# Sliding-window attention and a cosine-gated MLP on one core: the first pair of heads of q and k comes as f32 through SyncE's queue and is cast on chip

## Chip, cores and metric

One core of a Trainium2 chip runs the whole kernel. The metric is the device time of one execution in microseconds, lower is better: 307.88 us as the median of three runs of the kernel before (307.68 to 308.02).

## What is computed

Attention over 8 batches, 8 heads, 576 positions and 64 channels per head, causal, with a window of 64 positions; then an MLP on the 4608 tokens of 512 channels.

```python
scores = scale * np.matmul(q, k.transpose(0, 1, 3, 2))
mask = (rel >= 0) & (rel < window)            # rel = query position - key position, window = 64
attn = softmax(where(mask, scores, -1e9))
x = np.matmul(attn, v)  ->  [4608, 512]
h = x @ w_in                                  # 512 -> 2048
g = h * np.cos(h)
out = (g @ w_out).astype(np.float32)          # 2048 -> 512
```

All inputs are f32 in DRAM; the kernel computes in bf16 with f32 sums.

## The kernel before

**Two halves.** The MLP works on nine token tiles of 512 (`mt`); each needs 64 first-layer matmuls (L351) and 64 second-layer matmuls (L522). The attention for a batch is computed in units of 64 queries against 128 keys and is laid between the matmuls of the MLP, at places given by a plan of due times. Only the attention of batch 0 has nothing to hide behind: its steps are written out by hand in the string `FIRST` (L41 to L48) and are issued in that order, one after the other, each to its engine. Every engine then works through its own list in order, and waits where an operand isn't there yet. A schedule is not found by the compiler: the order in which the program is written is the order on each engine.

**The first stage.** The heads of batch 0 are taken in four pairs. A row tile `rows` holds q and k of batch 0 as bf16, 64 rows per head with nine positions each. For pair `p`, in the names of `FIRST`:

- `load_heads` (L140, DMA at L142) brings q or k of the pair from DRAM on GpSimd's queue. The source is f32 and the tile bf16, so this DMA casts on its way.
- `tq.p`, `tk.p` (L186): 18 small TensorE transposes each of q and k from `rows` into PSUM, through the identity `ident`.
- `pq.p`, `pk.p` (L197/L199 for q, L109 for k): the transposed rows are copied to the tile `T` by VectorE (d) or ScalarE (a).
- `s.p.g` (L238, L244): the scores of four units. One matmul puts the mask (`mask16` through `ident`, L238) into the PSUM bank, eight small ones add q times k (L244).
- `m` (L273, VectorE: row maximum), `e` (L288, ScalarE: four exponentials with their sums), `i` (L295, VectorE: reciprocal), `n` (L302, GpSimd or VectorE: normalisation), `w` (L311, TensorE: transposes of the weights), `c` (L109: copy of those), `v` (L330: weights times values), `x` (L109: copy to `xT`), `h` (L351: first matmuls of the MLP), `tb` (L346: ScalarE's table for the sine).

**The mask** is made on chip: GpSimd writes position differences by two iotas (`put_steps`, L115), VectorE makes the three mask pieces from them in five instructions (`put_masks`, L119 to L123; step `mk`), and ScalarE casts these to `mask16` in three (L125). Both parts of `mk` are therefore in the lists of VectorE and ScalarE ahead of the first `pq` and `pk`.

**The loads** before `FIRST` are in the order q and k of pair 0, the iotas, q and k of pairs 1, 2 and 3, and four pieces of v, all on GpSimd's queue. SyncE's queue carries no load: its first instruction in the kernel before is the DMA at L170, which copies values on chip for batch 1, at 45.8 us.

**Output buffers.** The pool `moe` has three buffers with the tag `out` (128 x 2 x 512 f32), for the results of the MLP (`out_sb`, L514). The first of them is needed when the second layer of token tile 0 is copied out.

The part that sets up the first stage (L447 to L457):

```python
    nc.vector.memset(small, 0.0)
    exp_table()
    make_identity(nc, ident)
    load_heads("q", 0, 0, 1)
    load_heads("k", 0, 0, 1)
    put_steps()
    for p0, n in ((1, 1), (2, 1), (3, 1)):
        for name in ("q", "k"):
            load_heads(name, 0, p0, n)
```

Of the kernel before, what the change touches and what calls it, by code (L numbers as in the profile page):

```python
# [14 lines left out]
F32 = mybir.dt.float32  # L15
# [15 lines left out]
RC = 9  # L31
# [20 lines left out]
def kernel(  # L52
# [9 lines left out]
    nc = tc.nc  # L62
    B, H, S, D = q.shape
    assert (B, H, S, D) == (8, 8, 576, 64)
    scale = 1.0 / math.sqrt(D)
    d_model = H * D
# [9 lines left out]
    moe = ctx.enter_context(tc.tile_pool(name="moe", bufs=2))  # L76
# [31 lines left out]
    def copy(engine, out, in_):  # L108
        {"a": nc.scalar.copy, "p": nc.gpsimd.tensor_copy}.get(engine, nc.vector.tensor_copy)(out, in_)  # L109
# [3 lines left out]
    def put_steps():  # L113
        for h in range(2):
            nc.gpsimd.iota(mask[64 * h:64 * h + 64, 0], pattern=[[2, 128]], base=-65, channel_multiplier=-2,  # L115
                           allow_small_or_imprecise_dtypes=True)
# [11 lines left out]
    def halves(tile_):  # L128
        return {name: tile_[:, i * PAIRS * S:i * PAIRS * S + PAIRS * S].rearrange("p (a x) -> p a x", a=PAIRS)
                for i, name in enumerate(("q", "k"))}  # L130

    def rows(b):
        return rowtiles[1 if b == 1 else 0]
# [6 lines left out]
    def load_heads(name, b, p0=0, n=PAIRS):  # L140
        src = {"q": q, "k": k}[name][b, 2 * p0:2 * p0 + 2 * n]
        nc.gpsimd.dma_start(out=halves(rows(b))[name][:, p0:p0 + n],  # L142
                            in_=src.rearrange("(a h) (p c) d -> (h p) a (c d)", h=2, c=RC))
# [198 lines left out]
    def exp_table():  # L342
        nc.scalar.activation(small, small, AF.Exp, scale=0.0)  # L343
# [45 lines left out]
    n = n_first  # L389
# [56 lines left out]

    nc.vector.memset(small, 0.0)  # L447
    exp_table()
    make_identity(nc, ident)
    load_heads("q", 0, 0, 1)  # L450
    load_heads("k", 0, 0, 1)
    put_steps()
    for p0, n in ((1, 1), (2, 1), (3, 1)):
        for name in ("q", "k"):
            load_heads(name, 0, p0, n)
    for c in range(4):
# [108 lines left out]
```

## Time and profile before

| | |
|---|---|
| median of three runs | 307.88 us (307.68 to 308.02) |
| the profiled execution, its own time | 308.04 us |
| its span (first to last instruction) | 306.0 us |
| TensorE matmul busy | 294.1 us, 96% of the span |
| ScalarE, VectorE, GpSimd busy | 235.6, 219.3, 171.9 us |
| first matmul starts | 4.82 us |
| first matmul of the MLP (`h.0`) | 21.68 us |
| start of the unbroken row of MLP matmuls (`h.2`) | 26.21 us |

The profile lists instructions by engine and by line of the kernel. "PE" is TensorE's matmul, "PEld" its weight load, "DVE" VectorE, "ACT" ScalarE, "POOL" GpSimd, "SP" SyncE. A row of the timeline has the start in us from the span's start, the busy time in us (instructions that follow each other directly are merged, with their count), engine, line, operation, output and input, and in brackets the idle time before it with what ended it. The chain of waits is the work that ended last, followed back from the last instruction to what released each step. Busy times of TensorE overlap a little, since matmuls are pipelined; where a step's length matters the distance from start to start is used.

### The profile page before, as it was taken

How to read it: one execution, taken by the hardware profiler on the slowest of the kernel's cores; microseconds unless marked ns; L12 is line 12 of the kernel's file. 1: busy time of each engine (PE TensorE's matmuls, PEld its weight loads, DVE VectorE, ACT ScalarE, POOL GpSimd, SP SyncE). 2: the span in 40 equal slices, each digit the busy share in tenths (PEclk: the TensorE clock that was granted, in tenths of full speed). 3: DMA queues.
4: the chain of work that ended last, by engine and by line, in shares of the span. 5: the costliest groups of instructions: out<-in, count | busy, mean ns of one | idle time of the engine just before them, and what ended most of it. 6: DMA issues, size and time to landing. Idle time of an engine off the chain costs nothing.

```text
span 306.0 us, 7884 instructions
## 1 busy us (share of the span) xinstructions
PE 294.1 (96%) x2668; PEld 143.1 (47%) x2668; DVE 219.3 (72%) x832; ACT 235.6 (77%) x786; POOL 171.9 (56%) x200
## 2 busy tenths in 40 slices
PE   3979999999999999999999999999999999999996
PEld 2645444444444444444454445444544454454443
DVE  2796889678787778777878787788778877235701
ACT  4798689977997799879986998699869987106600
POOL 8997237889465976497759765957533630000000
PEclk9989999999999999999999999999999999999999
DMA  6999999599969999999999999999993441011012
GB/s 83 167 211 207 208 168 161 79 179 166 238 110 159 180 197 135 164 149 219 145 170 161 213 141 170 161 216 120 171 170 117 88 130 61 0 72 70 0 69 71
DMA packets 165577, 43.58 MB, mean 142 GB/s; under 512 B 154720, under 2 KB 161056, under 8 KB 165536
## 3 DMA queue, kind: packets, MB, share of 16 engines
q0 software_dynamic: 99632, 18.36, 75.4%
q1 hardware_dynamic: 65760, 24.52, 39.9%
q8 instruction: 21, 0.34, 0.5%
q10 hardware_dynamic: 144, 0.20, 0.2%
q14 instruction: 20, 0.16, 0.2%
HBM read 36.70 MB, written 9.44 MB: 151 GB/s over the span
## 4 chain that ended last, share of the span: by engine, by line
PE 83%; ACT 5%; DVE 5%; DMA 3%; POOL 1%; issue 1%; POOLq 0%; DVEq 0%
PE h_ps L351 41%; PE out_ps L522 33%; ACT e L288 3%; PE o_ps L330 3%; PE s_ps L261 3%; DMA rows<-in_q_dram 1%; PE out_ps L366 1%; DVE s L277 1%; DMA wT<-w 1%; DVE negm L273 1%; DVE w L302 1%; ACT L343 1%; PE tk_ps L186 1%; PE tq_ps L186 1%; POOL w L302 1%
## 5 line engine op out<-in xcount | busy, mean ns | idle before, releaser
L351 PE MATMUL h_ps<-xT,w_in 128*128 128x512 bf16 x576 | 128.1, 381 | 0.9 <-ACT xT L109 0.5
L522 PE MATMUL out_ps<-w_out,gT 128*128 128x512 bf16 x560 | 125.1, 379 | 0.2 <-DVE gT L510 0.2
L510 DVE TENSOR_TENSOR gT<-h_ps,sin 128x512 bf16<-128x512 f32 x144 | 95.5, 689 | 35.4 <-ACT sin L507 35.2
L507 ACT ACTIVATE sin<-h_ps 128x512 f32<-128x512 f32 x144 | 83.0, 599 | 34.2 <-PE h_ps L351 33.0
L288 ACT ACTIVATE e<-s,negm 128x128 f32<-128x128 f32 x256 | 98.6, 387 | 0.3 <-DVE negm L277 0.3
L302 POOL TENSOR_TENSOR w<-e,rden 128x512 bf16<-128x512 f32 (+1 forms) x76 | 74.3, 992 | 32.4 <-DVE rden L295 30.3
L351 PEld LDWEIGHTS <-w_in 128*128 128x128 bf16 x576 | 55.9, 98 | 66.7 <-issue 2.0
L522 PEld LDWEIGHTS <-gT 128*128 128x128 bf16 x560 | 53.2, 98 | 62.4 <-issue 0.2
L277 DVE CUSTOM_DVE_ANT_0 s<-s_ps,mask 128x128 f32<-128x128 f32 x256 | 58.1, 285 | 0.4 <-PE s_ps L261 0.4
L288 ACT ACTIVATION_READ_ACCUMULATOR e<-s,negm 128x1 f32 x256 | 48.0, 188 | 0.0
L149 POOL DMA_DIRECT2D rows<-in_q_dram x30 | 25.4, 866 | 25.3 <-DMA T<-rows 15.5
L162 POOL DMA_DIRECT2D v<-in_v_dram x35 | 29.6, 869 | 12.4 <-DMA rows<-in_k_dram 5.8
L109 ACT COPY out_sb<-out_ps 128x512 f32<-128x512 f32 (+1 forms) x18 | 10.1, 561 | 24.4 <-PE out_ps L522 19.0
L295 DVE RECIPROCAL rden<-den 128x4 f32<-128x4 f32 (+1 forms) x80 | 13.8, 172 | 18.3 <-ACT e L288 17.1
L149 POOL DMA_DIRECT2D rows<-in_k_dram x30 | 25.5, 898 | 0.5 <-DMA T<-rows 0.5
L109 DVE CAST xT<-o_ps 128x512 bf16<-128x512 f32 x26 | 16.9, 681 | 6.5 <-PE o_ps L330 6.2
L277 DVE DVE_READ_ACCUMULATOR2_ANT negm<- 128x1 f32 x256 | 21.3, 83 | 0.0
L109 DVE COPY out_sb<-out_ps 128x512 f32<-128x512 f32 x18 | 12.4, 689 | 12.0 <-PE out_ps L522 12.0
L288 ACT ACTIVATE e<-s_ps,negm 128x128 f32<-128x128 f32 x32 | 11.4, 394 | 1.6 <-DVE negm L273 1.4
L261 PE MATMUL s_ps<-T 64*64 64x128 bf16 x512 | 12.1, 221 | 0.0
L261 PEld LDWEIGHTS <-T 64*64 64x64 bf16 x512 | 8.2, 106 | 8.3 <-DVE negm L277 3.9
L330 PEld LDWEIGHTS <-v 128*64 128x64 bf16 x504 | 9.7, 114 | 4.4 <-issue 2.3
(54 smaller groups left out, 148.9 us busy)
## 6 DMA issues: line engine op xcount, KB each, us to landing
out_dram<-out_sb SPq DMA_DIRECT2D x16, 512.0 KB, 6.9
v<-in_v_dram POOLq DMA_DIRECT2D x28, 128.0 KB, 8.3
rows<-in_q_dram POOLq DMA_DIRECT2D x24, 128.0 KB, 5.9
rows<-in_k_dram POOLq DMA_DIRECT2D x24, 128.0 KB, 9.0
w_out<-in_moe_w_out_dram POOLq DMA_DIRECT2D x2, 1024.0 KB, 16.8
w_in<-in_moe_w_in_dram POOLq DMA_DIRECT2D x2, 768.0 KB, 12.1
wT<-w SPq DMA_TRANSPOSE x66, 3.8
out_dram<-out_sb SPq DMA_DIRECT2D x3, 256.0 KB, 2.0
```

Source lines behind the costliest of these rows:

```text
L109: {"a": nc.scalar.copy, "p": nc.gpsimd.tensor_copy}.get(engine, nc.vector.tensor_copy)(out, in_)
L149: nc.gpsimd.dma_start(out=rows(b)[lo:lo + n, slot * 512:slot * 512 + 512].rearrange("p (h d) -> p h d", h=H), in_={"q": q, "k": k}[name][b ...
L162: nc.gpsimd.dma_start(out=vt.rearrange("p (h d) -> p h d", h=H), in_=v[b, :, c * 128:c * 128 + n, :].rearrange("h p d -> p h d"))
L261: nc.tensor.matmul(out=s_ps[cross][to, u].rearrange("p (a t) -> p a t", a=2), lhsT=q_cols(b, p, j)[d], rhs=k_cols(b, p, j)[d], start=True, ...
L277: nc.vector.tensor_tensor_reduce(out=s[:, u], in0=s_ps[:, u], in1=mask[:, 2 - j % 2 if j else 0], scale=-scale if b else -1.0, scalar=BIG, ...
L288: nc.scalar.activation(e[:, u], s[:, u], AF.Exp, bias=negm[:, u:u + 1], scale=1.0 if n < n_first else -1.0, accum_out=den[:, u:u + 1])
L302: (nc.gpsimd if engine == "p" else nc.vector).tensor_tensor(out=w[:, 0:u], in0=e[:, 0:u], op=ALU.mult, in1=rden[:, 0:u].unsqueeze(2).to_br ...
L330: nc.tensor.matmul(out=o_ps[64 * h:64 * h + 64, 64 * i:64 * i + 64], lhsT=values_of(b)[:, max(j - 1, 0), 128 * p + 64 * h:128 * p + 64 * h ...
L351: nc.tensor.matmul(out=st["h", ff], lhsT=w_in_sb[:, ks, ff * 128:ff * 128 + 128], rhs=st["xT", mt][:, ks], start=start, stop=stop)
L507: nc.scalar.activation(sin, h_ps, AF.Sin, bias=math.pi / 2.0)
L510: nc.vector.tensor_tensor(out=gt[:, e], in0=h_ps, in1=sin, op=ALU.mult)
L522: nc.tensor.matmul(out=o_ps[e], lhsT=gT[ff // 2][:, ff % 2, ms * 128:ms * 128 + 128], rhs=w_out_sb[:, ff], start=ff == 0, stop=ff == n_ff - 1)
```

## The change

Nothing of the computation changes. Four edits stand in one place, behind `exp_table()`:

- q and k of pair 0 no longer come through `load_heads`. SyncE issues two DMAs, ahead of everything else in its list, that bring the same rows as f32 into two of the three `out` buffers (`first_f32`, 576 f32 to a partition).
- ScalarE casts q, and VectorE casts k, from `first_f32` to the place in `rows` that the DMA filled before. Both casts come ahead of the mask's steps in the lists of these engines.
- GpSimd loads pair 1 where it loaded pair 0, and has two DMAs less in all; the iotas stay behind its second load.
- Pairs 2 and 3 follow the iotas directly.

```diff
     nc.vector.memset(small, 0.0)
     exp_table()
+    first_f32 = {}
+    for name, src in (("q", q), ("k", k)):
+        first_f32[name] = moe.tile([128, 2, d_model], F32, tag="out", name="first_f32", bufs=3).rearrange("p a b -> p (a b)")[:, 0:S]
+        nc.sync.dma_start(out=first_f32[name], in_=src[0, 0:2].rearrange("h (p c) d -> (h p) (c d)", c=RC))
     make_identity(nc, ident)
-    load_heads("q", 0, 0, 1)
-    load_heads("k", 0, 0, 1)
+    load_heads("q", 0, 1, 1)
+    load_heads("k", 0, 1, 1)
     put_steps()
-    for p0, n in ((1, 1), (2, 1), (3, 1)):
+    for name, engine in (("q", "a"), ("k", "d")):
+        copy(engine, halves(rows(0))[name][:, 0], first_f32[name])
+    for p0, n in ((2, 1), (3, 1)):
         for name in ("q", "k"):
             load_heads(name, 0, p0, n)
```

The beginning of VectorE's list, with the difference marked. The rows at L119 to L123 make the mask, `rows_72` is the tile of batch 0's rows, and the branch into the program differs by its line number alone:

```order
-L560 UNCONDITIONAL_BRANCH
+L566 UNCONDITIONAL_BRANCH
 L447 MEMSET small 128x1
+L109 CAST rows_72<-first_f_87 128x576
 L119 TENSOR_TENSOR mask<-mask 128x128
 L120 TENSOR_SCALAR mask<-mask 128x128
```

The cast of k now stands in front of all the mask's instructions. The beginning of ScalarE's list, with the load of its exponential table and the three casts to `mask16` (L125):

```order
 L343 ACT_TABLE_LOAD
 L343 ACTIVATE small<-small 128x1
+L109 CAST rows_72<-first_f_85 128x576
 L125 CAST mask_81<-mask 128x384
 L125 CAST mask_81<-mask 128x256
```

The cast of q stands between the table and the mask's casts. GpSimd's list around the iotas, where each line at L142 is the load of one pair's q or k:

```order
 L142 DMA rows_72<-in_k_dram 128x576
 L115 IOTA mask 64x128 x2
-L142 DMA rows_72<-in_q_dram 128x576
-L142 DMA rows_72<-in_k_dram 128x576
 L142 DMA rows_72<-in_q_dram 128x576
 L142 DMA rows_72<-in_k_dram 128x576
```

Two loads have gone behind the iotas, and what follows them comes two DMA issues sooner. SyncE's list gains its two DMAs at the front. TensorE's list keeps its order; only its first weight load now waits for ScalarE and not for a DMA.

## Prediction

> **What bounds the kernel now.** I first read the chain of waits by engine, to see whether TensorE sets the end, and then the same chain in order of time, to see where it does not. Times in the rows are us from the span's start.
>
> ```profile
> PE 83%; ACT 5%; DVE 5%; DMA 3%; POOL 1%; issue 1%; POOLq 0%; DVEq 0%
> ```
>
> ```profile
> 1.45 1.29 POOL rows L142 x2
> ...
> 3.25 4.54 DMA rows<-in_q_dram
> ...
> 9.80 0.56 PE s_ps L244 x8
> ...
> 12.97 0.58 PE s_ps L244 x8
> ...
> 13.58 0.69 DVE negm L273
> ...
> 21.68 1.44 PE h_ps L351 x3
> ...
> 26.21 5.77 PE h_ps L351 x26
> ```
>
> TensorE sets 83% of the span. From 26.21 on it has work without a break, in an order that the change leaves alone. So the change is worth as much as it moves that 26.21. The chain behind it is: the load of q of pair 1 (issued at 3.25 as GpSimd's third load, landed 4.54 later), `tq.1` at 7.83, TensorE until `s.1.1` ends at 13.5, then VectorE with no gap until `h.0` at 21.68. ScalarE runs beside it: it waits 1.08 before 10.88 (row below), and afterwards is full.
>
> The timeline to 11.5 shows the steps that the change touches:
>
> ```profile
> 0.74 1.28 ACT L343 ACT_TABLE_LOAD   x1 [0.74 <-PEq L549]
> 3.25 0.55 POOL L142 DMA_DIRECT2D rows<-in_q_dram  x1
> 3.33 0.29 DVE L119 TENSOR_TENSOR mask<-mask 128x128 f32<-128x128 f32 x1 [2.46 <-POOL mask L115]
> 4.34 0.11 DVE L123 MEMSET mask<- 128x64 f32 x1
> 4.54 1.02 ACT L125 CAST mask<-mask 128x384 bf16<-128x384 f32 x3 [2.30 <-DVE mask L123]
> 4.82 0.69 PE L186 MATMUL tq_ps<-ident,rows 64*64 64x64 bf16 x18 [4.82 <-DMA rows<-in_q_dram]
> 5.49 0.69 PE L186 MATMUL tk_ps<-ident,rows 64*64 64x64 bf16 x18
> 6.11 0.61 PE L238 MATMUL s_ps<-mask,ident 128*128 128x512 bf16 x1
> 6.22 0.64 ACT L109 COPY T<-tk_ps 128x576 bf16<-128x576 bf16 x1 [0.66 <-PE tk_ps L186]
> 6.91 0.63 PE L244 MATMUL s_ps<-T 64*64 64x128 bf16 x8 [0.19 <-ACT T L109]
> 7.83 0.69 PE L186 MATMUL tq_ps<-ident,rows 64*64 64x64 bf16 x18 [0.29 <-DMA rows<-in_q_dram]
> 10.88 0.65 ACT L197 ACTIVATE T<-tq_ps 128x576 bf16<-128x576 bf16 x1 [1.08 <-PE tq_ps L186]
> 11.43 0.36 ACT L288 ACTIVATE e<-s_ps,negm 128x128 f32<-128x128 f32 x1
> ```
>
> Three facts matter. TensorE waits 4.82 for q of pair 0. The mask is ready at 4.54 + 1.02 = 5.56, only 0.55 before L238 needs it, so the mask is second in line. And the 0.29 before 7.83 is pair 1 arriving late.
>
> **The change part by part: pair 0's landing.** The price of a SyncE load of f32 from DRAM stands nowhere. The nearest rows are SyncE's last stores, with nothing beside them, its copies on chip in the midst of other traffic, and the loads of pair 0 and its followers on GpSimd's queue (columns: transfer, queue, count, KB, median us from issue to landing); and one issue by SyncE.
>
> ```profile
> out_dram<-out_sb SPq DMA_DIRECT2D x3, 256.0 KB, 2.0
> v<-v SPq DMA_DIRECT2D x1, 256.0 KB, 6.2
> out_dram<-last_sb SPq DMA_DIRECT2D x1, 64.0 KB, 1.6
> ```
>
> ```profile
> rows<-in_q_dram POOLq DMA_DIRECT2D x1, 144.0 KB, 3.3
> ```
>
> ```profile
> 303.30 0.33 SPq L370 DMA_DIRECT2D out_dram<-last_sb  x1
> ```
>
> From 64 to 256 KB the stores grow by 0.4, 2.1 ns per KB. The f32 tile is 288 KB, so about 2.0 + 0.07 = 2.07. SyncE should begin with the others (ScalarE's first row starts at 0.74), so q lands at 0.75 + 2.07 = 2.8. k is issued 0.33 later, at 1.08, and would land at 3.15 if it had the queue to itself; behind q's 288 KB (0.6 at the same slope, less the 0.33) it is 3.4. I take q at 2.8 and **k at 3.4**. Bounds for k: 1.08 + 1.6 = 2.7, and 1.08 + 6.2 = 7.3; the second is a copy amid full traffic, which the beginning doesn't have:
>
> ```profile
> 0.00:2.60 2.60, 0.00 (x0) 0.00 (x0) 0.06 (x1) 1.49 (x2) 1.86 (x8) 1.00 0.00 0
> 2.60:3.80 1.20, 0.00 (x0) 0.00 (x0) 0.43 (x2) 0.00 (x0) 1.14 (x5) 1.00 0.70 82
> ```
>
> The last two columns (share of the DMA engines, GB/s) are zero until 2.6, so SyncE's loads begin on idle engines and meet pair 1's loads only at their end.
>
> [...]
>
> **The casts.** Rows for both engines, f32 from SBUF (ScalarE's gives min, median and max in ns, VectorE's the mean in ns after the busy us):
>
> ```profile
> L125 ACT CAST mask<-mask x3: 293/400/512, 4.5 to 5.3; 128x384 bf16<-128x384 f32 x1, 128x256 bf16<-128x256 f32 x1, 128x128 bf16<-128x128 f32 x1
> ```
>
> ```profile
> L120 DVE TENSOR_SCALAR mask<-mask 128x128 f32<-128x128 f32 x1 | 0.2, 227 | 0.0
> L122 DVE COPY mask<-mask 128x64 f32<-128x64 f32 x1 | 0.2, 196 | 0.0
> ```
>
> ```profile
> L109 DVE COPY T<-tk_ps 128x576 bf16<-128x576 bf16 x3 | 2.3, 752 | 0.0
> ```
>
> ScalarE grows by 0.86 ns per element (293 at 128, 512 at 384), so 576 take 0.68. VectorE grows by 0.48 (196 at 64, 227 at 128), so 576 take 0.44; the upper bound is the 0.75 of the same width from PSUM. I take 0.45.
>
> **The new beginning.** q cast: 2.85 to 3.53 (ScalarE has its table since 2.02). `tq.0` at 3.6 instead of 4.82, `tk.0` ends 0.67 + 0.69 later, at 4.9. That 1.2 is *not* what is gained, since the cast of k stands ahead of the mask. k cast: 3.45 to 3.9, behind it VectorE's mask row, which took 4.45 − 3.33 = 1.12: 3.93 to 5.05, instead of 4.45. ScalarE's casts follow 0.09 later and take 1.02: ready at 6.16 instead of 5.56. `pk.0` then starts at 6.18 (before 6.22), the scores of L244 0.69 later at 6.87 (before 6.91). So TensorE waits for the mask from 4.9 to 6.2, and the first score comes when it came before. What does go is the wait behind it: pair 1 now lands where pair 0 did, 3.3 after issues at 1.45 and (in the middle of the 1.29 that the two take) about 2.1, by 5.5. `tq.1` follows L244's eight by their 0.56 in the chain: 7.43 instead of 7.83, a **gain of 0.4**.
>
> In general `tq.1` starts at k's landing + k's cast + 3.56 (0.04 + 1.14 + 0.09 + 1.02 + 0.02 + 0.69 + 0.56), and it pays as long as landing plus cast is below 4.27. If k lands by 2.9 the mask is no longer held up, and `pk.0` follows at 5.58: gain 1.0 at most (0.64 from the mask's 5.56, and the 0.36 behind L244).
>
> **What carries the 0.4 on.** Three rows from the end of the stage:
>
> ```profile
> 18.52 1.48 DVE L109 COPY v<-v 64x1536 bf16<-64x1536 bf16 x1
> ...
> 19.51 0.40 PE L311 MATMUL tw_ps<-ident,w 128*128 128x128 bf16 x4 [1.48 <-POOL w L302]
> ...
> 23.59 0.58 ACT L109 COPY wT<-tw_ps 128x512 bf16<-128x512 bf16 x1 [0.48 <-PE tw_ps L311]
> ```
>
> From `tq.1` to `s.1.1` TensorE has no gap, and pairs 2 and 3 are issued two DMAs (twice 0.55, so 1.1) earlier than before, so it isn't stopped by them. ScalarE's `pq.2` at 10.88 waits for `tq.2`, and from `e.0.0` at 11.43 ScalarE has no idle time until the 0.48 before 23.59, so until 23.11; it moves by 0.4 as one piece. VectorE's row from 13.58 starts when `s.1.1` ends, 0.4 earlier too. GpSimd has its two issues less and so 1.1 of slack; its `n.1.1`, for which TensorE waited 1.48 at 19.5, comes earlier, but VectorE was busy until 20.0 anyway (`z.0`), so I price that at nothing; without that cover it would be another 0.5 to 1. Two of the three output buffers are taken, but free again from 3.9, some 40 us ahead of their first use. SyncE has nothing else to do in the whole stage. The w_in pieces come earlier, not later. Sum: 308.04 − 0.4 = 307.64 for the profiled execution, which stood 0.16 above the median; on the median's footing **307.5**.
>
> **Rivals.** *The clock.* The same 18 transposes take 0.69 before 13.3 and less after it, and three MLP matmuls at 21.68 take 1.44 (26 take 5.77 later, 0.22 each):
>
> ```profile
> 13.33 0.49 PE L186 MATMUL tq_ps<-ident,rows 64*64 64x64 bf16 x18
> ```
>
> ```profile
> 6.60:10.00 3.40, 2.88 (x52) 2.00 (x53) 2.13 (x4) 1.76 (x9) 3.37 (x4) 1.00 1.08 159
> 10.00:13.40 3.40, 3.40 (x64) 2.40 (x62) 2.19 (x5) 2.52 (x13) 3.23 (x4) 1.00 2.04 163
> ...
> 16.80:20.20 3.40, 1.92 (x37) 1.16 (x35) 3.40 (x7) 3.40 (x20) 3.32 (x3) 1.00 1.18 215
> 20.20:23.70 3.50, 3.25 (x40) 1.98 (x37) 3.09 (x8) 2.91 (x16) 3.48 (x5) 0.51 1.15 208
> ```
>
> So TensorE was slow until about 13.4 (the clock's column, third from the right, shows 1.00 there; the durations say otherwise), fast after 3.4 us that it filled, and slow again (0.51) for 3.5 after 3.4 that it filled only to 1.92. Without the wait before 7.83, it fills the stretch 6.6 to 10.0, and might be fast 3.4 sooner. VectorE then gets `s.1.1` about 1 earlier; ScalarE, which still starts `e.0.0` on `m.0.0`, only about 0.5 to 0.6. The gain above that lies at the end: ScalarE's last copy at 23.59 waited 0.48 for slow TensorE work (it was free at 23.11). Together 0.9: **307.0**. The same price covers k landing by 2.9. [...]
>
> *k comes late (the slower side).* The cast of k holds the mask, and the mask all scores. If a load by SyncE takes the 3.3 of GpSimd's load, k lands at 4.4; with the cast, `tq.1` comes at 8.4, 0.6 later: 308.5; with the cast at 0.75, 308.8. It decides from landing plus cast over 4.27. For it: both loads share the engines with pair 1 from 2.6. [...] Against: they start on idle ones.
>
> *Nothing arrives.* The 0.4 is used up further on, where VectorE and ScalarE run neck and neck from 13.6 to 21.7, or by the slow stretch at 20.3 staying put and covering more of `h.0`: 307.9.
>
> **How the numbers follow.** A gain of 0.1 to 0.6, the forecast, 0.44; the clock or an early k (307.0) 0.31; late k 0.17; nothing 0.08. About 0.2% (0.62 us, below 307.26 or above 308.50) is what a measurement here can tell. Faster by that: most of the second case and a little of the first, 0.33; slower: most of the third, 0.16; within, the rest, 0.51. The range reaches to both sides: 306.6 (the 1.0 with some of the clock) to 308.6. The forecast's own range is 307.2 to 307.8.
>
> **What would show it.** First, the cast of k's start: below 3.8 it pays. `tq.0` near 3.6, then a gap in TensorE of about 1.3 before L238 at 6.2 that is ended by ScalarE's mask cast; no DMA wait before `tq.1`, at 7.4; `h.2` at 25.8. If `tq.1` has moved and `h.2` hasn't, my carrying on is wrong; if transposes before 13 take 0.5, the clock decided; if L238 starts after 6.9, k was late.

## The result, and the profile after

The changed kernel took **306.57 us** (median of 22 runs, 306.17 to 308.42), the kernel before 307.99 beside it (22 runs): a ratio of 0.9961 [0.9949, 0.9973], so 1.2 us less, with 0.8 to 1.6 in the interval. The profiled execution took 306.21 (span 304.3), 1.83 less than that of before, so part of its difference is the execution's own. The runs of one kernel spread by 1 to 2 us with the course of TensorE's clock, which differs between runs (a mean of 0.989 to 1.00 in the changed kernel's): where its mean was 1.00, the kernel before took 307.51 (mean of 18 runs, taken beside the experiments) and the changed one 306.32 (mean of 9), again 1.2.

The chain of waits by engine, and five pieces of the same chain in order of time:

```profile
PE 87%; ACT 6%; DVE 3%; DMA 1%; issue 1%; POOL 0%; SPq 0%; DVEq 0%; POOLq 0%; ACTq 0%
```

```profile
1.20 3.14 DMA first_f<-in_k_dram
...
5.94 1.02 ACT mask L125 x3
...
11.41 4.19 ACT e L288 x24
...
23.19 1.28 ACT L346
...
25.21 5.77 PE h_ps L351 x26
```

The chain now begins with the load of k, goes through the mask, and reaches `h.2` at 25.21, where it was 26.21: 1.00 earlier. From `pq.2` at 10.76 to 25.16 it is ScalarE's list, which has no wait in all that time. Its first pieces are the ones that I had worried about. Rows from the first 8 us of the changed kernel:

```profile
0.75 0.39 SPq L452 DMA_DIRECT2D first_f<-in_q_dram  x1
1.20 0.42 SPq L452 DMA_DIRECT2D first_f<-in_k_dram  x1
3.68 0.67 ACT L109 CAST rows<-first_f 128x576 bf16<-128x576 f32 x1 [1.43 <-DMA first_f<-in_q_dram]
4.36 0.46 DVE L109 CAST rows<-first_f 128x576 bf16<-128x576 f32 x1 [3.48 <-DMA first_f<-in_k_dram]
4.40 0.69 PE L186 MATMUL tq_ps<-ident,rows 64*64 64x64 bf16 x18 [4.40 <-ACT rows L109]
5.74 0.11 DVE L123 MEMSET mask<- 128x64 f32 x1
5.94 1.02 ACT L125 CAST mask<-mask 128x384 bf16<-128x384 f32 x3 [1.59 <-DVE mask L123]
6.86 0.63 ACT L109 COPY T<-tk_ps 128x576 bf16<-128x576 bf16 x1
7.01 0.59 PE L238 MATMUL s_ps<-mask,ident 128*128 128x512 bf16 x1 [1.44 <-ACT mask L125]
7.54 0.63 PE L244 MATMUL s_ps<-T 64*64 64x128 bf16 x8
7.95 0.71 PE L186 MATMUL tq_ps<-ident,rows 64*64 64x64 bf16 x18
```

k landed at 1.20 + 3.14 = 4.34, its cast held up the mask, TensorE waited 1.44 for that, and `tq.1` (last row) came at 7.95, **0.12 later than before**. By the part of the program that the prediction priced, the change should have lost a little. Where it won shows in GpSimd's list (and, in this one execution, in TensorE's clock as well; the iotas below tell the two apart). The timeline of GpSimd from the w_in loads to the last normalisation of batch 0, first of the kernel before:

```profile
10.11 1.50 POOL L175 DMA_DIRECT2D w_in<-in_moe_w_in_dram  x2
11.67 1.04 POOL L302 TENSOR_TENSOR w<-e,rden 128x512 bf16<-128x512 f32 x1
...
14.95 1.08 POOL L302 TENSOR_TENSOR w<-e,rden 128x512 bf16<-128x512 f32 x1
16.09 2.25 POOL L109 COPY v<-v 64x2048 bf16<-64x2048 bf16 x1
18.42 3.21 POOL L302 TENSOR_TENSOR w<-e,rden 128x512 bf16<-128x512 f32 x3
...
22.55 1.06 POOL L302 TENSOR_TENSOR w<-e,rden 128x512 bf16<-128x512 f32 x1
```

and of the changed kernel:

```profile
8.93 1.56 POOL L175 DMA_DIRECT2D w_in<-in_moe_w_in_dram  x2
10.81 1.04 POOL L302 TENSOR_TENSOR w<-e,rden 128x512 bf16<-128x512 f32 x1 [0.32 <-DVE rden L295]
...
14.09 1.08 POOL L302 TENSOR_TENSOR w<-e,rden 128x512 bf16<-128x512 f32 x1
15.23 2.33 POOL L109 COPY v<-v 64x2048 bf16<-64x2048 bf16 x1
17.64 3.21 POOL L302 TENSOR_TENSOR w<-e,rden 128x512 bf16<-128x512 f32 x3
...
21.77 1.06 POOL L302 TENSOR_TENSOR w<-e,rden 128x512 bf16<-128x512 f32 x1
```

In both, the list shows no wait from GpSimd's first load at 1.45 to the last of these rows, but for one of 0.32 in the second. (The page's busy share doesn't show it, since DMA issues aren't counted as busy.) Two issues less put the w_in rows 1.18 earlier, the new wait takes 0.32 of it, and the rest stays with every row down to the last normalisation, `n.3.0`: 22.55 to 21.77, **0.78 earlier**. TensorE waits for these rows: its wait of 1.48 before `w.1.1` at 19.51 is now one of 1.16 at 18.74, 0.77 earlier.

### The profile page after: what moved, and what is told of

The parts are those of the page before. It is cut to its first block, busy times and chain, and to the rows that moved or that the text cites. A ratio compares the mean times of both kernels' runs of the same rounds, so it can differ in the third digit from the quotient of the medians.

```text
span 304.3 us, 7887 instructions
## 1 busy us (share of the span) xinstructions
PE 291.6 (96%) x2668; PEld 141.7 (47%) x2668; DVE 218.5 (72%) x833; ACT 235.8 (77%) x787; POOL 171.1 (56%) x198
## 4 chain that ended last, share of the span: by engine, by line
PE 87%; ACT 6%; DVE 3%; DMA 1%; issue 1%; POOL 0%; SPq 0%; DVEq 0%; POOLq 0%; ACTq 0%
PE h_ps L351 41%; PE out_ps L528 37%; ACT e L288 4%; PE o_ps L330 3%; PE s_ps L261 3%; PE out_ps L366 1%; DMA first_f<-in_k_dram 1%; DVE s L277 1%; PE tq_ps L186 1%; ACT wT L109 0%; DVE w L302 0%; PE tk_ps L186 0%; DVE out_sb L109 0%; ACT L343 0%; ACT L346 0%
```

## The experiments

Four theories, with the letters that the expectations use. *First scores* (A): the stage is set by the arrival of the first pairs, `tq.1` above all (the prediction's). *The clock* (B): TensorE runs at full speed in other stretches than before. *GpSimd's list* (C): the two issues that GpSimd no longer makes. And, once two loads put back had cost the whole gain, *traffic* (D): the bytes of these loads, not their issues. Extra loads, iotas and matmuls of the experiments write tiles that nobody reads. "Ratio" is to the kernel before on the same chip, with its 95% interval.

**First scores: the mask ahead of the cast.** In the changed kernel the cast of k moves behind the mask's five instructions on VectorE.

```diff
-    "tq.0 mk tk.0 pq.0.d pk.0.a s.0.1 tq.1 tk.1 l s.0.0 m.0.1 pq.1.d tq.2 e.0.1 pk.1.d s.1.0 pq.2.a "
+    "tq.0 mk kc tk.0 pq.0.d pk.0.a s.0.1 tq.1 tk.1 l s.0.0 m.0.1 pq.1.d tq.2 e.0.1 pk.1.d s.1.0 pq.2.a "
-    for name, engine in (("q", "a"), ("k", "d")):
-        copy(engine, halves(rows(0))[name][:, 0], first_f32[name])
+    copy("a", halves(rows(0))["q"][:, 0], first_f32["q"])
...
+             "kc": lambda: copy("d", halves(rows(0))["k"][:, 0], first_f32["k"]),
```

> The changed kernel with one thing moved: VectorE's cast of k stands behind the five mask instructions instead of ahead of them. Theory A (the mask's row behind k's cast set the first scores): the mask is ready near 5.6 instead of 6.96, the first L244 starts near 6.4 instead of 7.54, tq.1 at the landing of pair 1 near 7.0 instead of 7.95, and h.2 follows by 0.5 to 0.9, for 305.6 to 306.1 us. Rival B (only TensorE's clock decides, the beginning is hidden): tq.1 moves as said, but the time stays within 0.3 of the changed kernel's 306.57. Rival C (the two loads fewer on GpSimd's queue give the gain): as B.

Measured 306.09, ratio 0.9939 [0.9926, 0.9952]. Three rows of its timeline:

```profile
6.35 0.63 PE L244 MATMUL s_ps<-T 64*64 64x128 bf16 x8 [0.16 <-ACT T L109]
...
15.35 0.40 PE L311 MATMUL tw_ps<-ident,w 128*128 128x128 bf16 x4 [1.76 <-POOL w L302]
...
21.67 1.06 POOL L302 TENSOR_TENSOR w<-e,rden 128x512 bf16<-128x512 f32 x1
```

The first scores come 1.19 sooner than in the changed kernel (`tq.1` at 6.73, 1.22 sooner), the end only 0.5 (0.7 by the ratios). TensorE gives the rest back as a wait of 1.76 for GpSimd, whose last row gains 0.10. So 1.2 at the first scores is worth some 0.5 to 0.7 here, and 0.12 lost there nearly nothing.

**The clock.** Small matmuls of the identity fill TensorE's gaps ahead of `tq.0`, `s.0.1` and `w.1.1`: 30, 1 and 18 in the kernel before (below; `g` is the step `warm`), 26, 12 and 18 in the changed one.

```diff
-    "tq.0 mk tk.0 pq.0.d pk.0.a s.0.1 tq.1 tk.1 l s.0.0 m.0.1 pq.1.d tq.2 e.0.1 pk.1.d s.1.0 pq.2.a "
+    "g.30.X1 tq.0 mk tk.0 pq.0.d pk.0.a g.1.X1 s.0.1 tq.1 tk.1 l s.0.0 m.0.1 pq.1.d tq.2 e.0.1 pk.1.d s.1.0 pq.2.a "
...
-    "s.3.0 s.3.1 c.0.1.d n.1.1.p c.0.0.d w.1.0 m.3.0 i.2.0 z.0.d c.1.0.a n.2.0.p w.1.1 c.1.1.d v.0 "
+    "s.3.0 s.3.1 c.0.1.d n.1.1.p c.0.0.d w.1.0 m.3.0 i.2.0 z.0.d c.1.0.a n.2.0.p g.18.X0 w.1.1 c.1.1.d v.0 "
...
+    def warm(n, which):
+        t = bank(which, "warm_ps")
+        for _ in range(n):
+            nc.tensor.matmul(out=t[:, 0:128], lhsT=ident, rhs=ident, start=True, stop=True, skip_group_check=True)
```

> The kernel before, with 49 matmuls of the identity by itself (128 wide, results unused) laid where TensorE waits: 30 ahead of tq.0, 1 ahead of s.0.1, 18 ahead of w.1.1. They remove no load and no cast. Rival B (the clock): TensorE is at full speed from about 8 on and stays there, transposes take 0.45 to 0.5 us per 18 instead of 0.69, the slow stretch at 20.3 is gone, and the time falls by 0.9 to 1.5, to 306.5 to 307.1, with less spread. Theory A or rival C: TensorE's speed is hidden behind ScalarE and VectorE, 307.7 to 308.0.

> The changed kernel with 56 such matmuls: 26 ahead of tq.0, 12 ahead of s.0.1, 18 ahead of w.1.1. If the clock (B) is the whole difference, it stands within 0.3 us of the kernel before with the same filling, and its slower runs near 308.2 vanish. If the two loads fewer (C) count, it is 0.5 to 1 faster than that kernel. By A it is 0.1 slower than that kernel, since tq.1 is 0.12 later.

The kernel before with them: 308.25, ratio 1.0009 [0.9997, 1.0021]. Four rows of its timeline:

```profile
8.02 0.47 PE L186 MATMUL tq_ps<-ident,rows 64*64 64x64 bf16 x18 [0.94 <-DMA rows<-in_q_dram]
8.76 0.69 PE L186 MATMUL tk_ps<-ident,rows 64*64 64x64 bf16 x18 [0.27 <-DMA rows<-in_k_dram]
...
22.45 1.06 POOL L302 TENSOR_TENSOR w<-e,rden 128x512 bf16<-128x512 f32 x1
...
122.67 0.47 PE L330 MATMUL o_ps<-wT,v 128*64 128x64 bf16 x18 [0.46 <-DMA wT<-w]
```

Its transposes take 0.47 already at 8.0 (0.69 without the matmuls) and the slow stretch at 20.3 is gone (granted clock 1.00 from 20.2 to 23.7, where the kernel before had 0.51), but another has come in its place: the next transposes, at 8.76, take 0.69 again, and the granted clock is 0.79 from 6.6 to 10.0 and 0.70 from there to 13.4. GpSimd's last row moves by 0.10. `h.2` comes 0.64 earlier, at 25.57, yet nothing is gained at the end: in this execution TensorE waits 0.46 for a transfer of `wT` at 122.67, where the kernel before had no such wait. Whether the other runs lose it there too isn't known. The changed kernel with them: 306.82, ratio 0.996 [0.9948, 0.9972], all five runs at a granted clock of 1.0. The two differ by 1.4, and by 1.0 where the clock was full in both (307.72, two of the twelve runs, against 306.73), so the clock isn't what the change gained by.

**Two loads put back.** In the changed kernel GpSimd loads pair 0 as well, into a spare tile, behind the iotas.

```diff
     put_steps()
+    spare = const.tile([128, 2, S], BF16, name="spare")
+    for i in range(2):
+        nc.gpsimd.dma_start(out=spare[:, i], in_=(q, k)[i][0, 0:2].rearrange("h (p c) d -> (h p) (c d)", c=RC))
```

> The changed kernel with two more GpSimd loads behind the iotas (q and k of pair 0 into a tile that nobody reads), so that GpSimd has its old number of issues and its queue the old bytes. C: GpSimd's work is 1.1 later, n.1.1 and w_in with it, and the time goes back by 0.5 to 1, to 307.1 to 307.6. B and A: the time stays within 0.3 of 306.57; pairs 2 and 3 land 1.1 later but still ahead of tq.2.

Measured 308.20, ratio 1.0002 [0.9991, 1.0014]: the whole gain is gone, with `tq.1` where the change has it (7.98). GpSimd's last normalisation starts at 22.95. This fits its list, and traffic as well. Two kernels take these apart.

**Traffic without GpSimd, GpSimd without traffic.** Both in the changed kernel: two more f32 loads of 288 KB by SyncE into a spare tile; or four iotas on GpSimd ahead of the loads of v, which move no byte.

```diff
+    spare = const.tile([128, 2, S], F32, name="spare")
+    for i in range(2):
+        nc.sync.dma_start(out=spare[:, i], in_=(q, k)[i][0, 0:2].rearrange("h (p c) d -> (h p) (c d)", c=RC))
```

```diff
+    spare = const.tile([128, 2, 128], F32, name="spare")
+    for i in range(4):
+        h = i % 2
+        nc.gpsimd.iota(spare[64 * h:64 * h + 64, i // 2], pattern=[[2, 128]], base=-65, channel_multiplier=-2,
+                       allow_small_or_imprecise_dtypes=True)
```

> The changed kernel with two more f32 loads of 288 KB by SyncE, behind the first two, into a tile that nobody reads: more bytes in the queues, GpSimd's list as in the changed kernel. Theory C: within 0.4 of 306.57, pair 1's landing a little later. Rival D (what the two extra GpSimd loads cost was their traffic, not GpSimd's time): 307.5 to 308.3.

> The changed kernel with four more iotas of 64x128 on GpSimd (about 0.27 us each, 1.1 in all) ahead of the loads of v, into a tile that nobody reads: GpSimd's time as before the change, no bytes more. Theory C: back to 307.6 to 308.2. Rival D (traffic) and B (clock): within 0.3 of 306.57.

The iotas: 307.91, ratio 0.9993 [0.9978, 1.0009], the gain gone without a byte. Its rows on GpSimd:

```profile
5.49 1.07 POOL L465 IOTA spare<- 64x128 f32 x4
...
11.62 1.04 POOL L302 TENSOR_TENSOR w<-e,rden 128x512 bf16<-128x512 f32 x1
...
18.36 3.22 POOL L302 TENSOR_TENSOR w<-e,rden 128x512 bf16<-128x512 f32 x3
...
22.50 1.06 POOL L302 TENSOR_TENSOR w<-e,rden 128x512 bf16<-128x512 f32 x1
```

From 11.62 on they stand within 0.06 of those of the kernel before, while `tq.1` stays at 7.91. So 1.07 of GpSimd's time costs 1.3 by the medians, and 0.9 where the mean clock was 1.00 (307.26, four runs, against 306.32; the kernel before took 307.35 there on the same chip): the change's gain, within the intervals. This run decides for GpSimd's list.

A row of ScalarE, ahead of its exponentials `e.3.1`, shows one way in which the list acts:

```profile
21.08 0.37 ACT L288 ACTIVATE e<-s_ps,negm 128x128 f32<-128x128 f32 x1 [0.32 <-DVE negm L273]
```

In the changed kernel ScalarE has no wait here. Now it waits 0.32 for the row maximum `m.3.1`, which VectorE makes behind `z.0`, and `z.0` ends only after GpSimd's `n.1.1` (see the next section). `h.2` starts at 25.62, 0.41 later than in the changed kernel. The kernel before without its slow stretch (the one with idle matmuls) has the same list and nearly the same `h.2`, 25.57. By these four executions, then, about 0.4 of the 1.00 that `h.2` gained is GpSimd's list, and 0.6 the slow stretch, which comes and goes between executions. At the row of 59 MLP matmuls that begins the next token tiles (62.13 before, 61.50 with the idle matmuls, 61.54 with the iotas, 60.77 changed) it is about 0.75 and 0.6 of 1.36.

SyncE's extra loads took 308.18, ratio 1.0004 [0.9991, 1.0016], where that theory expected no loss. One row says how they act:

```profile
8.68 1.76 POOL L162 DMA_DIRECT2D v<-in_v_dram  x2 [1.44 <-DMA rows<-in_q_dram]
```

GpSimd's issue of a piece of v waits 1.44 for the landing of the load of q made eight issues earlier, which lands late beside the added traffic, and everything behind it moves: `n.3.0` starts at 22.97. Traffic costs here too, through the same list; it also delays `tq.1`, to 8.44.

**Shorter lists in the kernel before.** If GpSimd's issues alone count, taking some away without SyncE's loads should gain too. (The rival, E in the expectations: the scores and ScalarE's list are as long as GpSimd's, and shortening that alone gives nothing.) Pairs 2 and 3 in one load each of q and k; or two pieces of w_in in one load.

```diff
-    for p0, n in ((1, 1), (2, 1), (3, 1)):
+    for p0, n in ((1, 1), (2, 2)):
```

```diff
-    loads = iter([(load_w_in, 0, 512), (load_w_in, 512, 1280), (load_w_in, 1280, 2048),
+    loads = iter([(load_w_in, 0, 512), (load_w_in, 512, 2048), (lambda: None,),
```

> The kernel before, with the loads of pairs 2 and 3 put together: GpSimd issues two loads of two pairs each instead of four of one. No load by SyncE, no cast on an engine, the same bytes. Theory C (GpSimd has no idle time from 1.45 on, so its list sets the first stage): GpSimd's list is about 0.9 to 1.0 shorter, w of n.1.1 and h.2 come 0.7 to 1.0 earlier, 306.9 to 307.3 us. Theory A (the first scores set it) or B (the clock): 307.8 to 308.1, since the first scores do not move; tq.2 might even wait for the larger load.

> The kernel before, with the second and third load of w_in put together: one GpSimd issue (about 0.75 to 0.8 us) less in front of n.0.0, nothing else moved; the loads ahead of it and their landings stay. Theory C (GpSimd's list sets the first stage): n.0.0 waits for i.0.0 and starts near 14.4 instead of 14.95, n.1.1 near 17.8 instead of 18.4, and the time falls by 0.5 to 0.7, to 307.3 to 307.5. Rival E (the scores and ScalarE are as long as GpSimd's list, so that shortening GpSimd alone gives nothing): 307.8 to 308.1.

Neither gained, and the first lost: 309.02, ratio 1.0028 [1.001, 1.0045], and 307.89, ratio 0.9998 [0.9983, 1.0013]. The rows say why; of the first:

```profile
9.31 0.69 PE L186 MATMUL tk_ps<-ident,rows 64*64 64x64 bf16 x18 [0.53 <-DMA rows<-in_k_dram]
...
15.43 1.03 POOL L302 TENSOR_TENSOR w<-e,rden 128x512 bf16<-128x512 f32 x1 [1.03 <-DVE rden L295]
17.07 2.12 POOL L109 COPY v<-v 64x2048 bf16<-64x2048 bf16 x1 [0.61 <-DMA v<-in_v_dram]
```

and of the second:

```profile
16.71 1.89 POOL L109 COPY v<-v 64x2048 bf16<-64x2048 bf16 x1 [1.17 <-DMA v<-in_v_dram]
```

The time that GpSimd saved it spent waiting. Beside the bigger loads others land later: in the first kernel pair 1's k (5.5 us on its way, before 4.7; `tk.1` at 9.31, before at 8.57), and in both v, for which GpSimd's copy waits 0.61 and 1.17 (in the second, two of its pieces took 7.4 us for 6.4 before). So the theory needs its condition: fewer issues gain only as long as what GpSimd then works on is there.

**The same on top of the change.** The w_in pieces merged in the changed kernel; the pairs, or the w_in pieces, merged in the kernel with the mask first; and that kernel with 34 of the idle matmuls ahead of `w.0.0` and `w.1.1`.

> The changed kernel with the same merging. Its n.0.0 starts at 14.09 and i.0.0 ends at 13.9, so GpSimd can only come 0.2 earlier: theory C gives 306.2 to 306.6, near the changed kernel's 306.57. If GpSimd's list were the only bound, 305.8.

> The changed kernel with the mask ahead of k's cast and with the loads of pairs 2 and 3 put together. Theory C with ScalarE as the next bound: GpSimd's n.0.1 then waits for i.0.1, so that only part of the further 1.0 is kept: 305.2 to 305.8. If GpSimd were still the only bound: 305.0. If the larger load makes tq.2 wait (landing near 9.5): 306.0 to 306.6.

> The changed kernel with the mask ahead of k's cast and the same merging. There TensorE waited 1.76 for n.0.0, and i.0.0 was done 0.6 ahead of it: theory C gives 0.4 to 0.7 below that kernel's 306.09, so 305.4 to 305.7. Rival E: 305.9 to 306.2.

> The changed kernel with the mask ahead of k's cast and 34 idle matmuls of the identity in TensorE's two waits for GpSimd (20 ahead of w.0.0, 14 ahead of w.1.1). B in a smaller part (the slow stretch costs what runs at clock 0.989 show over 1.0, some 0.7): 305.6 to 305.8, no slow stretch. If GpSimd's list hides it: 306.0 to 306.3.

| kernel | us | ratio |
|---|---|---|
| change, w_in merged | 307.69 | 0.9988 [0.9974, 1.0002] |
| mask first, pairs merged | 305.97 | 0.9941 [0.992, 0.9962] |
| mask first, w_in merged | **305.84** | 0.9929 [0.9916, 0.9941] |
| mask first, idle matmuls | 306.39 | 0.9944 [0.9931, 0.9957] |

The w_in pieces merged cost the change 1.1. With the mask first they cost nothing: that kernel has the lowest median of all here, 0.25 below the mask first alone (306.09), which is within the intervals and less than the 0.4 to 0.7 expected. First the change with w_in merged (two rows of GpSimd, with one of VectorE between them):

```profile
14.79 1.89 POOL L109 COPY v<-v 64x2048 bf16<-64x2048 bf16 x1
14.97 2.25 DVE L302 TENSOR_TENSOR w<-e,rden 128x512 bf16<-128x512 f32 x1
...
19.31 2.13 POOL L302 TENSOR_TENSOR w<-e,rden 128x512 bf16<-128x512 f32 x2 [0.81 <-DVE rden L295]
```

and the mask first with w_in merged:

```profile
13.05 1.06 POOL L302 TENSOR_TENSOR w<-e,rden 128x512 bf16<-128x512 f32 x1
...
20.93 1.05 POOL L302 TENSOR_TENSOR w<-e,rden 128x512 bf16<-128x512 f32 x1
```

In the first, GpSimd's copy now starts 0.18 ahead of VectorE's normalisation, which then takes 2.25 (in the changed kernel it starts 0.10 ahead of the copy and takes 0.68); the reciprocals behind it are late, and GpSimd waits 0.78 and 0.81 for them. With the mask first they are there in time, and the list ends 0.84 before the change's. Pairs merged gained nothing over the mask first alone, and neither did the idle matmuls, with the clock at 1.0 all along.

All 14 kernels together, by the start of `n.3.0` and of `tq.1` in the profiled execution:

| kernel | `tq.1` | `n.3.0` | that execution, us | median, us |
|---|---|---|---|---|
| before | 7.83 | 22.55 | 308.04 | 307.99 |
| change | 7.95 | 21.77 | 306.21 | 306.57 |
| mask first | 6.73 | 21.67 | 306.52 | 306.09 |
| before, idle matmuls | 8.02 | 22.45 | 308.10 | 308.25 |
| change, idle matmuls | 7.76 | 21.46 | 306.65 | 306.82 |
| two loads back | 7.98 | 22.95 | 308.20 | 308.20 |
| before, pairs merged | 8.09 | 23.41 | 308.75 | 309.02 |
| SyncE traffic | 8.44 | 22.97 | 307.87 | 308.18 |
| GpSimd iotas | 7.91 | 22.50 | 307.28 | 307.91 |
| mask first, pairs merged | 6.87 | 21.77 | 306.67 | 305.97 |
| before, w_in merged | 7.99 | 22.81 | 308.01 | 307.89 |
| change, w_in merged | 8.01 | 22.36 | 307.33 | 307.69 |
| mask first, w_in merged | 6.63 | 20.93 | 305.76 | 305.84 |
| mask first, idle matmuls | 6.85 | 21.75 | 306.49 | 306.39 |

A line through `n.3.0` leaves 0.3 us (root mean square) of the profiled times, with 1.23 us of the end for 1 us of `n.3.0`; a line through `tq.1` leaves 0.6, and misses the changed kernel by 1.4. The first line is no proof by itself, since `n.3.0` stands late in the stage and moves with much that delays it; the iotas are.

## Why the prediction was right and wrong

It forecast a small gain, 307.5, and a small gain came, three times as large and from another place: 306.57 lies below the forecast's own 307.2 to 307.8 and at the lower end of the range, 306.6. That the sign came true was luck, since the term that was to give the gain lost 0.12. Point by point:

- **GpSimd's two issues less: the step that failed.** The prediction had them, 1.1 us, and said "I price that at nothing", since "VectorE was busy until 20.0 anyway (`z.0`)"; its price without that cover was 0.5 to 1. They are worth the gain (iotas: 307.91 against 306.57). The cover was GpSimd's own doing. `z.0` takes 1.48 in the kernel before, where it starts 0.10 behind GpSimd's `n.1.1`, and 0.65 to 0.75, about half of that, in four kernels where it starts ahead. In the changed kernel it starts 0.09 behind (VectorE's two rows):

```profile
17.73 1.49 DVE L109 COPY v<-v 64x1536 bf16<-64x1536 bf16 x1
19.17 0.42 DVE L109 COPY wT<-tw_ps 128x512 bf16<-128x512 bf16 x1
```

  In the kernel with two loads back it starts 0.20 ahead:

```profile
18.41 0.67 DVE L109 COPY v<-v 64x1536 bf16<-64x1536 bf16 x1
...
20.41 0.42 DVE L109 COPY wT<-tw_ps 128x512 bf16<-128x512 bf16 x1 [1.34 <-PE tw_ps L311]
```

  In this kernel VectorE is done early and then waits 1.34 for `w.1.1`, which waits for `n.1.1`: the same end of the same GpSimd instruction, shown once as a long copy and once as idle time. So VectorE was not busy until 20.0; it stood behind GpSimd, and moved with it. Nor was ScalarE without idle time from 11.43 to 23.11, as the prediction read it. Each exponential starts 0.09 after the start of the instruction that reads the sum of the one ahead, but before the change `e.1.1` (14.30) started 0.23 after it and `e.3.1` (21.13) 0.42. The wait ahead of `e.3.1` is the one that the iotas bring back.

  Which of the two starts first shows on both. Before, where GpSimd starts first, `z.0` ended 0.51 after `n.1.1` (20.00 against 18.42 + 1.07), a little less than the 0.65 to 0.75 that it takes when it starts ahead: nearly as if it had waited for `n.1.1`. Where `z.0` starts first, GpSimd loses less: with the mask first and idle matmuls, `n.1.1` starts 0.08 behind `z.0`, which has 0.57 to go, and `w.1.1` follows 1.27 after it, where it is 1.09 in the kernel before. The rows don't show what holds either of them; the reason is open.
- **The landing: mis-sized.** 2.07 us for a SyncE load of 288 KB, from the stores, was 2.9 and 3.14; k at 4.34 in place of 3.4. The casts were right (0.67 and 0.46 for 0.68 and 0.45). Pair 1, forecast by 5.5, landed near 7.0 (k: issued at 2.18, 4.8 on its way), still ahead of `tk.1`. The term that was to give 0.4 gave −0.12.
- **The late k.** Its sign came true (L238 at 7.01, after 6.9), its loss did not. `tq.1` came at 7.95 in place of the rival's 8.4, since the steps from the end of k's cast took 3.13 and not 3.56 (the mask row and `pk.0` each began 0.08 to 0.10 before the instruction ahead of them ended, and L244's eight took 0.41 to the next start and not 0.56); and a late `tq.1` costs little while GpSimd's list is what is waited for. (`tk.0` would have ended at 4.96 by the prediction's own terms, not at 4.9; nothing hangs on it.)
- **That 26.21 sets the end** held in part only: `h.2` moved by 1.00, the end of the span by 1.7, and in the kernel before with idle matmuls `h.2` moved by 0.64 and the end not at all. By the row of 59 matmuls the change had gained 1.36. GpSimd's first normalisation for batch 1 also comes 1.0 earlier (49.93 to 48.92), and a wait of 0.18 of TensorE for it at 52.19 is gone; that the rest comes from there is argued and wasn't tried.
- **The clock** changed in part as the rival said (18 transposes take 0.49 and not 0.69 from 11.62 on, before from 13.33, which is 1.7 sooner and not 3.4; no slow stretch at 20.3 in this execution, with a granted clock of 1.00 from 20.2 to 23.7). It is some 0.6 of what the profiled executions differ by, but it isn't the gain: that is 1.2 at a full clock too, and the idle matmuls gained nothing in three kernels.

What stays open: the part of the 1.2 that comes behind `h.2`, where GpSimd's list had given 0.4, and behind the row of 59, where it had given 0.75; and why `h.2` alone is worth so little: the idle matmuls moved it 0.64, 0.27 and 0.49 earlier in the three profiled executions, and the end didn't follow.

## What to carry to other kernels

An engine whose rows follow each other without a bracket can be the bound of its stage, whatever its busy share says: DMA issues are work of their engine, and 1.1 us of them less gave the gain. Before an engine's busy time is taken as a cover, see whether its long instruction is long everywhere: if its length depends on when another engine starts, as that of `z.0` did (0.67 or 1.49), the cover goes when that engine goes. And a shorter list pays only until the next operand is late: one issue less cost the changed kernel 1.1, and no longer cost anything once the mask came first.

## What the runs showed of the hardware

Two loads of 288 KB f32 by SyncE, issued at 0.75 and 1.20 while the DMA engines moved nothing (0 GB/s to 1.6), took 2.9 and 3.1 us from issue to landing, against 2.0 for its stores of 256 KB. Beside them GpSimd's first load of 144 KB took 4.7, where it took 3.3 in the kernel before; the transfers of the changed kernel (KB, median us):

```profile
first_f<-in_q_dram SPq DMA_DIRECT2D x1, 288.0 KB, 2.9
first_f<-in_k_dram SPq DMA_DIRECT2D x1, 288.0 KB, 3.1
...
rows<-in_q_dram POOLq DMA_DIRECT2D x1, 144.0 KB, 4.7
```

VectorE's and GpSimd's rows are longer or shorter with the order of their starts: VectorE's bf16 copy of 64x1536 took 0.65 to 0.75 when it started ahead of GpSimd's multiplication (mask first 0.75, two loads back 0.67, change with w_in merged and mask first with idle matmuls 0.65) and 1.36 to 1.49 when it started 0.09 to 0.23 behind it (mask first with pairs merged 1.36, before and change with idle matmuls 1.48, change 1.49), and its normalisation took 2.25 behind GpSimd's copy (0.68 at its shortest); GpSimd's copy took 1.89 at its shortest and 1.96 to 2.33 where it started while VectorE's normalisation ran. In two kernels an issue by GpSimd waited for the landing of the load eight issues before it (1.44 with SyncE's extra traffic, 0.23 with two loads back).
